# First MLP's output product with half of its k-tiles by Strassen, and a list scheduler for all work behind attention

## The chip, the cores and the metric

The kernel runs on one core of a Trainium2 chip. The metric is device time of one execution in microseconds (us). Of the core's engines five matter here: TensorE (PE in the rows; the weight loads that it does beside its matmuls are PEld), VectorE (DVE), ScalarE (ACT) and SyncE (SP), whose queue issues nearly all transfers from and to the chip's memory (DMA). GpSimd (POOL) does almost nothing.

## The reference, cut to what matters

Attention with a sigmoid in place of a softmax, then two MLPs. Tokens: 2 x 448 = 896; model width 768; the first MLP is 1536 wide, the second 2048.

```python
attn = 1 / (1 + exp(-(q @ k.T / 8 - log(448))))      # 2 x 12 heads, 448 x 64 each
x    = (attn @ v), heads side by side                 # 896 x 768
xn   = x / sqrt(mean(x * x) + 1e-6) * rms_g
h    = silu(xn @ w_gate) * (xn @ w_val)               # 896 x 1536
y    = h @ w_out                                      # 896 x 768   <- the product that changes
g    = silu(y @ w_in)                                 # 896 x 2048
out  = g @ w_out2                                     # 896 x 768
```

## The kernel before

**Numbers.** Every fp32 operand is held as two parts of TensorE's faster fp32 form, high and low. A high part is a copy on ScalarE (`high`, L132), a low part a subtraction on VectorE (`low`, L135). One tile product is three passes (`PASSES`): high x high, high x low, low x high. Activations lie with features on the 128 partitions and the 896 tokens along the row, so that one matmul has 128 x 128 weights and 448 moving columns (one half b of the tokens).

**Weights.** They lie in the chip's memory as 64-bit floats, 6 (in the last product 5) tiles of 128 x 128 to a slab. `load_next` (L124) brings a slab into one of two `raw` buffers. `front` (L137) makes a 32-bit float of it: ScalarE takes the upper word (L145), VectorE or ScalarE the upper bits of the lower word (L151 or L148), VectorE merges them (L153). `back_std` (L160) makes high and low parts in one of 4 `ring` buffers. `back_mac` (L173) does it for two slabs that a Strassen product uses: four sums of blocks (L180, L182, L192, L196) and 3.5 slabs of high and low parts.

**Strassen.** A call of `strassen` (L363) makes two output tiles (256 features) from 6 k-tiles with 7 groups of 9 matmuls (`group`, L346; matmuls on L350) where the plain form has 72. The groups are A11, S1, S2, A12, S3, S4, A22; they use three PSUM banks x, y, z. Between them ScalarE saves partial sums (L380, L382, L385) and VectorE adds them (L372): S2 can write bank x when the first save is done, S3 when the third save is, and A22 when VectorE has added the result of S3. The activations come in seven forms, four blocks (three of them used alone) and four differences of blocks T1 to T4, each again high and low.

**Stages behind attention.** (1) g and v: gate and value of the first MLP, pair by pair; the results are the six h tiles. (2) o: the first MLP's output product, plain, `duo` and `product` (L310, matmuls on L321), 6 output tiles with 12 k-tiles each. (3) i: the second MLP's input product, the pair i0 plain, the pairs i1 to i7 by Strassen. (4) e: the output product, three pairs, each with 6 of 16 k-tiles by Strassen and 10 plain (`mixed`, L405).

**What sets the order.** Each engine runs its instructions in the order in which the program issues them. TensorE's are issued as the loops above stand. VectorE's and ScalarE's side work comes from two sources, the stream of weight steps (`stream`, L247) and a list `fore` of activation work. After each tile or group `pump` (L285) issues from them in turn, as long as a running sum of VectorE's costs stays behind a running sum of TensorE's; the outputs of the products are issued at their place in the loops. ScalarE's costs are not counted. Factors (`PACE_I` and so on) stretch VectorE's costs stage by stage.

Of the kernel before, what the change touches and what calls it, by code (L numbers as in the profile page):

```python
# [21 lines left out]
P = 128  # L22
# [10 lines left out]
PACE_I = 0.85  # L33
PACE_E = 0.85
PACE_M = 1.0
PACE_L = 1.5
POLITE_E = False
# [5 lines left out]
ORDER = (0, 2, 4, 1, 3, 5)  # L43


@with_exitstack
def tile_attention_two_mlps(
# [9 lines left out]

# [30 lines left out]
    items += [("std", first + s) for s in range(KD * K1 // 6)]  # L106
    first += KD * K1 // 6
# [11 lines left out]
    live = {"ring": 0, "w4": 0, "f": 0}  # L119
# [3 lines left out]

    def load_next():  # L124
        if order:
            s = order.pop(0)
            raws[s] = wraw.tile([P, 2 * SLAB], U32, tag="raw", name=f"raw{s}")
            n = 2 * wide(s)
            nc.sync.dma_start(raws[s][:, :n], wd[s].bitcast(U32)[:, :n])
# [7 lines left out]
    def front(s, act_z):  # L137
        while live["f"] >= 3:
            yield None
        yield 0.0  # L140
        live["f"] += 1
        words = raws.pop(s)[:, : 2 * wide(s)].rearrange("p (n two) -> p n two", two=2)
        f = floats[s] = wf.tile([P, SLAB], F32, tag="f", name=f"f{s}")[:, : wide(s)]
        fu = f.bitcast(U32)
        nc.scalar.activation(f, words[:, :, 1].bitcast(F32), AF.Prelu, scale=2.0**-112, alpha=2.0**32)  # L145
        z = words[:, :, 0]
        if act_z:
            nc.scalar.activation(z.bitcast(I32), z, AF.Copy, scale=2.0**-29 * (1 - 2.0**-18), bias=-0.5 + 2.9e-5)  # L148
        else:
            yield 0.56  # L150
            nc.vector.tensor_scalar(z, z, 29, None, ALU.logical_shift_right)  # L151
        yield 0.96
        nc.vector.scalar_tensor_tensor(fu, fu, 3, z, ALU.logical_shift_left, ALU.bitwise_or)  # L153
        load_next()

    def slot(kind, most):
        while live[kind] >= most:
            yield None

    def back_std(s):  # L160
        yield from slot("ring", RING)
        yield 0.0
        live["ring"] += 1
        t = ring.tile([P, 2, SLAB], F32R, tag="w", name=f"w{s}")
        f = floats.pop(s)
        n = wide(s)
        high(t[:, 0, :n], f)
        yield 0.96
        low(t[:, 1, :n], f, t[:, 0, :n])
        live["f"] -= 1  # L170
        wt[s] = t

    def back_mac(s):  # L173
        f, g = floats.pop(s), floats.pop(s + 1)
        a11, a12, a21, a22 = f[:, :HALF], f[:, HALF:], g[:, :HALF], g[:, HALF:]
        tt = nc.vector.tensor_tensor
        yield 0.56
        sums = wsum.tile([P, SLAB], F32, tag="s", name=f"s{s}")
        s1, s2 = sums[:, :HALF], sums[:, HALF:]
        tt(s1, a21, a22, ALU.add)  # L180
        yield 0.56
        tt(s2, s1, a11, ALU.subtract)  # L182
        w = []
        for n in range(2):
            yield from slot("ring", RING)
            yield 0.0
            live["ring"] += 1
            w.append(ring.tile([P, 2, SLAB], F32R, tag="w", name=f"w{s}_{n}"))
            high(w[n][:, 0], (f, sums)[n])
            if n == 0:  # L190
                yield 0.56
                tt(a21, a11, a21, ALU.subtract)  # L192
                yield 0.96
                low(w[0][:, 1], f, w[0][:, 0])
                yield 0.56
                tt(a12, a12, s2, ALU.subtract)  # L196
        yield from slot("ring", RING)
        yield 0.0
        live["ring"] += 1
        w.append(ring.tile([P, 2, SLAB], F32R, tag="w", name=f"w{s}_2"))  # L200
        high(w[2][:, 0], g)
        yield 0.96
        low(w[1][:, 1], sums, w[1][:, 0])
        yield from slot("w4", 1)
        yield 0.0
        live["w4"] += 1
        w4 = wsum.tile([P, 2, HALF], F32R, tag="w4", name=f"w{s}_3")
        high(w4[:, 0], a12)
        yield 0.96
        low(w[2][:, 1], g, w[2][:, 0])  # L210
        yield 0.56
        low(w4[:, 1], a12, w4[:, 0])
        live["f"] -= 2
        wt[s] = {
            "A11": w[0][:, :, :HALF],
            "A12": w[0][:, :, HALF:],
            "S1": w[1][:, :, :HALF],
            "S2": w[1][:, :, HALF:],
            "S3": w[2][:, :, :HALF],
            "A22": w[2][:, :, HALF:],  # L220
            "S4": w4,
        }

    def alternate(a, b):

        gens = [[g, next(g, StopIteration)] for g in (a, b) if g is not None]
        gens = [e for e in gens if e[1] is not StopIteration]
        i = 0
        while gens:
            i %= len(gens)  # L230
            for j in range(len(gens)):
                e = gens[(i + j) % len(gens)]
                if e[1] is None:
                    e[1] = next(e[0])
                if e[1] is not None:
                    break
            else:
                yield None
                continue
            yield e[1]  # L240
            e[1] = next(e[0], StopIteration)
            i = gens.index(e) + 1
            if e[1] is StopIteration:
                gens.remove(e)
                i -= 1

    def stream():  # L247
        before = None
        for kind, s in items:
            act_z = kind == "mac" and s < 2 * K1  # L250
            yield from alternate(front(s, act_z), before)
            if kind == "mac":
                yield from front(s + 1, act_z)
            before = (back_mac if kind == "mac" else back_std)(s)
        yield from before

    steps = stream()
    head = [next(steps)]
    fore, turn, polite, pace = [], [True], [False], [1.0]
    spare = []  # L260

    def unblocked():
        return not fore[0][2:] or bool(spare)

    clock = {"pe": 0.0, "dve": 0.0}

    def step():

        if head[0] is None:
            head[0] = next(steps, StopIteration)  # L270
        can = head[0] is not None and head[0] is not StopIteration
        if fore and unblocked() and not (can and (polite[0] or turn[0])):
            turn[0] = True
            cost, do = fore.pop(0)[:2]
            clock["dve"] += cost * pace[0]
            do()
            return True
        turn[0] = False
        if not can:
            return False  # L280
        clock["dve"] += head[0] * pace[0]
        head[0] = next(steps, StopIteration)
        return True

    def pump():  # L285
        clock["dve"] = max(clock["dve"], clock["pe"] - 3.0)
        while True:
            ahead = [c for c in (fore[0][0] if fore and unblocked() else None, head[0]) if c not in (None, StopIteration)]
            if ahead and clock["dve"] + min(ahead) > clock["pe"]:
                return  # L290
            if not step():
                return

    def evac(cost):
        clock["dve"] = max(clock["dve"], clock["pe"]) + cost

    def until(ready):
        while not ready():
            assert step()

    def weights(s):
        until(lambda: s in wt)
        return wt[s]

    def done(s, n=1):
        live["ring"] -= n
        del wt[s]


    def product(ps, tiles, acts, bs, last=True, after=None, first=True, final=True):  # L310

        n = len(tiles)
        ps = ps if isinstance(ps, list) else [ps[:, b, :S] for b in range(2)]
        for i, (w, a) in enumerate(zip(tiles, acts)):
            s, o = divmod(w, 6)
            fin = o == wide(s) // P - 1
            until(lambda: a in act)
            t, x = weights(s)[:, :, o * P : (o + 1) * P], act[a]
            for step_, (jw, jx) in enumerate(PASSES):
                for b in bs:  # L320
                    nc.tensor.matmul(  # L321
                        ps[b],
                        t[:, jw],
                        x(jx)[:, b * S : (b + 1) * S] if len(x(jx).shape) == 2 else x(jx)[:, b],
                        start=(first and i == 0 and step_ == 0),
                        stop=(final and i == n - 1 and step_ == 2),
                        skip_group_check=True,
                    )
            clock["pe"] += 0.2027 * 3 * len(bs)
            if last and fin:  # L330
                done(s)
# [724 lines left out]
```

## Time and profile before

| what | value |
|---|---|
| time, median of 3 runs | 547.66 us (547.58 to 549.15) |
| the profiled execution's own time | 548.62 us |
| its span, first to last instruction | 546.4 us |
| TensorE busy | 541.0 us, 99% |
| VectorE busy | 388.3 us, 71% |
| ScalarE busy | 315.6 us, 58% |
| DMA, mean over the span | 119 GB/s |
| granted clock of TensorE | 0.999 of full |

The chain that ended last is TensorE for 97% of the span. In the rows below a matmul's own duration is longer than the distance to the next one, since matmuls are pipelined; VectorE's and ScalarE's rows overlap a little in the same way. What an instruction costs its engine is therefore read from start to start.

### The profile page before, as it was taken

What the parts mean: (1) busy time and instruction counts of PE and PEld (TensorE: products, weight loads), DVE (VectorE), ACT (ScalarE), POOL (GpSimd) and SP (SyncE); (2) the same over time, 40 slices, a digit from 0 to 9 for tenths busy, and PEclk for the clock granted to TensorE, in tenths of its full rate; (3) what the DMA queues carried; (4) which work ended last, traced back from release to release, by engine and by line L of the source; (5) the groups of instructions that cost most, each with busy time, mean ns of one, the idle gap of its engine ahead of it and who ended that gap; (6) DMA issues with size and microseconds to landing.
All of it is one profiled execution on the core that took longest, in us unless ns stands there. A gap on an engine that the chain in (4) does not pass through costs nothing.

```text
span 546.4 us, 7105 instructions
## 1 busy us (share of the span) xinstructions
PE 541.0 (99%) x2785; PEld 468.8 (86%) x2785; DVE 388.3 (71%) x589; ACT 315.6 (58%) x438; POOL 0.2 (0%) x4
## 2 busy tenths in 40 slices
PE   8999999999999999999999999999999999999997
PEld 4555459999999999999999999999999899999996
DVE  4576777897777877899563587599989995835610
ACT  5887773656757585757353355577767945223400
POOL 0000000000000000000000000000000000000000
PEclk9999999999999999999999999999999999999999
DMA  8855100443333333335533330233333443714201
GB/s 277 287 176 161 58 1 0 140 150 115 117 116 116 116 116 115 117 115 175 173 116 115 116 116 6 111 115 116 116 108 101 150 152 107 244 47 128 83 22 47
DMA packets 15521, 65.00 MB, mean 119 GB/s; under 512 B 1984, under 2 KB 3776, under 8 KB 15488
## 3 DMA queue, kind: packets, MB, share of 16 engines
q1 hardware_dynamic: 15344, 64.32, 35.7%
q8 instruction: 22, 0.36, 0.3%
q10 hardware_dynamic: 144, 0.23, 0.1%
q14 instruction: 11, 0.09, 0.1%
HBM read 61.79 MB, written 2.75 MB: 118 GB/s over the span
## 4 chain that ended last, share of the span: by engine, by line
PE 97%; ACT 1%; DMA 1%; issue 0%; DVE 0%
PE o L321 16%; PE av L533 7%; PE sc L517 6%; PE v L321 5%; PE g L321 3%; PE i L321 3%; PE e0b L321 2%; PE e1b L321 2%; PE e1a L321 2%; PE e0a L321 2%; PE e0x L350 1%; PE i6x L350 1%; PE e2x L350 1%; PE i3x L350 1%; PE v3x L350 1%; PE i5x L350 1%
## 5 line engine op out<-in xcount | busy, mean ns | idle before, releaser
L132 ACT ACTIVATE w<-f 128x768 fp32r<-128x768 f32 (+2 forms) x89 | 67.5, 762 | 66.5 <-PE o L321 22.7
L135 DVE TENSOR_TENSOR w<-f,w 128x768 fp32r<-128x768 f32 (+2 forms) x89 | 74.2, 849 | 40.9 <-ACT w L132 40.9
L153 DVE SCALAR_TENSOR_TENSOR f<-f,raw 128x768 uint32<-128x768 uint32 (+1 forms) x70 | 65.3, 932 | 19.7 <-ACT raw L148 14.0
L145 ACT ACTIVATE f<-raw 128x768 f32<-128x768 f32 (+1 forms) x70 | 61.4, 888 | 25.6 <-DMA raw<-in_w 20.6
L321 PE MATMUL o<-hhi,w 128*128 128x448 f32 x288 | 70.2, 365 | 0.0
L321 PEld LDWEIGHTS o<-hhi,w 128*128 128x128 f32 x288 | 54.1, 188 | 4.3
L525 ACT ACTIVATE a<-sc,logs 112x896 f32<-112x896 f32 x48 | 45.0, 1012 | 6.0 <-PE sc L517 5.7
L321 PE MATMUL o<-hlo,w 128*128 128x448 f32 x144 | 40.9, 365 | 0.0
L533 PE MATMUL av<-a,vr 112*64 112x448 f32 x192 | 39.4, 547 | 0.0
L517 PEld LDWEIGHTS sc<-ks 64*112 64x112 f32 x288 | 25.5, 181 | 14.2 <-ACT a L525 8.5
L517 PE MATMUL sc<-ks 64*112 64x448 f32 x288 | 35.0, 388 | 0.6 <-ACT ks L507 0.6
L321 PE MATMUL v<-x,w 128*128 128x448 f32 x144 | 29.9, 368 | 0.0
L533 PEld LDWEIGHTS av<-a,vr 112*64 112x64 f32 x192 | 12.3, 136 | 20.3 <-issue 18.2
L151 DVE TENSOR_SCALAR raw<-raw 128x768 uint32<-128x768 uint32 (+1 forms) x52 | 28.1, 540 | 2.0 <-DMA raw<-in_w 1.9
L321 PEld LDWEIGHTS v<-x,w 128*128 128x128 f32 x144 | 27.1, 188 | 2.5 <-issue 0.4
L321 PEld LDWEIGHTS o<-hlo,w 128*128 128x128 f32 x144 | 27.1, 188 | 2.1
L132 ACT ACTIVATE w<-s 128x768 fp32r<-128x768 f32 x19 | 16.0, 841 | 10.2 <-PE o L321 4.8
L135 DVE TENSOR_TENSOR w<-s,w 128x768 fp32r<-128x768 f32 x19 | 18.0, 949 | 3.1 <-ACT w L132 3.1
L148 ACT ACTIVATE raw<-raw 128x768 int32<-128x768 uint32 x18 | 16.1, 897 | 0.0
L321 PE MATMUL g<-x,w 128*128 128x448 f32 x72 | 15.3, 369 | 0.0
L321 PEld LDWEIGHTS g<-x,w 128*128 128x128 f32 x72 | 13.4, 188 | 1.8 <-issue 0.7
L321 PE MATMUL i<-y,w 128*128 128x448 f32 x72 | 14.8, 365 | 0.0
(443 smaller groups left out, 1051.5 us busy)
## 6 DMA issues: line engine op xcount, KB each, us to landing
raw<-in_w SPq DMA_DIRECT2D x58, 768.0 KB, 4.3
raw<-in_w SPq DMA_DIRECT2D x12, 640.0 KB, 3.9
kq<-in_kq SPq DMA_DIRECT2D x11, 448.0 KB, 6.0
vr<-in_v SPq DMA_DIRECT2D x12, 224.0 KB, 4.8
out_t<-e0s SPq DMA_DIRECT2D x4, 224.0 KB, 3.0
out_t<-e1s SPq DMA_DIRECT2D x4, 224.0 KB, 1.9
out_t<-e2s SPq DMA_DIRECT2D x4, 224.0 KB, 1.9
kq<-in_kq ACTq DMA_DIRECT2D x1, 224.0 KB, 3.5
```

The lines of the kernel that those rows point to most:

```text
L132: nc.scalar.activation(dst, src, AF.Copy)
L135: nc.vector.tensor_tensor(dst, src, hi.bitcast(F32), ALU.subtract)
L145: nc.scalar.activation(f, words[:, :, 1].bitcast(F32), AF.Prelu, scale=2.0**-112, alpha=2.0**32)
L148: nc.scalar.activation(z.bitcast(I32), z, AF.Copy, scale=2.0**-29 * (1 - 2.0**-18), bias=-0.5 + 2.9e-5)
L151: nc.vector.tensor_scalar(z, z, 29, None, ALU.logical_shift_right)
L153: nc.vector.scalar_tensor_tensor(fu, fu, 3, z, ALU.logical_shift_left, ALU.bitwise_or)
L321: nc.tensor.matmul(ps[b], t[:, jw], x(jx)[:, b * S : (b + 1) * S] if len(x(jx).shape) == 2 else x(jx)[:, b], start=(first and i == 0 and s ...
L350: nc.tensor.matmul(ps, w[a][:, jw, t * P : (t + 1) * P], forms(b, t, jx), start=(start and t == 0 and n == 0), stop=(stop and t == 2 and n ...
L517: nc.tensor.matmul(ps[:CP, h, :S], ks[i][rows, jk, 0, c * CP : (c + 1) * CP], ks[i][rows, jq, 1, :], start=(step == 0), stop=(step == 2),)
L525: nc.scalar.activation(a, ps[:CP, :, :S], AF.Sigmoid, bias=logs[:CP], scale=D**-0.5)
L533: nc.tensor.matmul(ps[h * D : (h + 1) * D], vr[i][:, c, h, :], a[:, h, :], start=(c == 0), stop=(c == NC - 1),)
```

## The change

**The product o** is now made like e: `mixed` is called for three pairs of output tiles with h tiles 0 to 2 (6 k-tiles) by Strassen and h tiles 3 to 5 (6 k-tiles) plain. For the first two pairs the plain part comes first, for the third it comes last. The three h tiles need their blocks and differences (`formed`: 5 high parts, 5 low parts and 4 subtractions where a plain tile has 2 and 2), and six of o's slabs go through the Strassen form of the weights. The outputs are added into the fp32 tiles `yr` (`dest`), and `y_put` makes high and low parts from there, half by half.

**The order** is no longer made by `pump`. Everything behind attention becomes a `Job` with an engine, a cost, its inputs and what it takes from a stock (ring buffers, PSUM banks and so on). `Plan.run` walks through time with one queue per engine: TensorE's jobs keep their order, every other engine takes the startable job with the earliest due date, which is worked back from when TensorE would need its result. The costs are formulas of the row length. The slabs' bit step is on ScalarE for o as well now (`ZO`). Activation tiles come from one store that is given back half by half. In attention itself only the names and homes of small tiles change, and two weight steps less are done there. SyncE's queue has the same 70 slab loads and 12 output transfers as before, in nearly the same sequence.

```diff
-    pair = duo("o", w0, K1, "h")
-    for m in range(2, KD):
-        product(ps, range(w0, w0 + K1), [("h", k) for k in range(K1)], (0, 1), after=after)
-        collected(m, ps, [(both, ps[:, :, :S])])
+    keys = [("h", k) for k in range(6, K1)]
+    for t in range(3):
+        dest = lambda m, b, t=t: r2[t]()[:, b, m]
+        if t < 2:
+            weight_std(s, ZO)
+            weight_std(s + 1, ZO)
+            weight_mac(s + 2, ZO)
+            mixed(f"o{t}", s + 2, s, keys, 6, hbook, hdep, y_put(t), dest)
+        else:
+            weight_mac(s, ZO)
+            weight_std(s + 2, ZO)
+            weight_std(s + 3, ZO)
+            mixed(f"o{t}", s, s + 2, keys, 6, hbook, hdep, y_put(t), dest, ahead=False, own=hown)
+        s += 4
...
+LAG = {"A": 0.105, "D": 0.081, "P": 0.165, "S": 4.4}
+HOP = 0.6
...
+    def dve(n, fn, deps=(), **more):
+        return plan.add("D", 0.071 + n / 960, fn, deps, **more)
+    def scalar(n, fn, deps=(), psum=False, **more):
+        return plan.add("A", (0.072 if psum else 0.109) + n / 1215, fn, deps, **more)
+    def tensor(n, fn, deps=(), **more):
+        return plan.add("P", 0.2027 * n, fn, deps, **more)
...
+    def run(self, busy):
...
+        t = 0.0
+        for j in self.pe:
+            j.due = t
+            t += j.cost
+        for j in reversed(self.jobs):
+            if j.eng != "P":
+                j.due = min([u.due for u in j.users + j.users_of_gift], default=1e9) - j.cost - LAG[j.eng] - HOP
...
+        def pick(e, now):
...
+            for j in sorted(pool[e], key=lambda j: j.due):
+                if not startable(j, now):
+                    continue
+                late = now + j.cost
+                if any(now < u.ready < late and u.due + drift < late and u.due < j.due for u in pool[e]):
+                    continue
+                return j
...
+    def y_put(t):
+        def put(m, b, src, dep):
...
+            l = dve(S, lo_, [scalar(S, hi_, [dep], need=some)])
...
+            if len(ydone[t]) == 4:
+                turned("y", t, r2[t], ydone[t], ybook[t], ydep[t], yown[t])
...
+    def formed(key, q, tile_, deps, book, fdep, own):
...
+        for name, src in (("B11", b11), ("B21", b21), ("B22", b22)):
...
+            h_ = scalar(S, raw, deps, need=some)
+            lows.append(dve(S, raw_low, [h_]))
...
+        t1, t2, t3, t4 = differences(blocks, lows)
...
+        ls = split(f"{key}{q}t", srcs, [[t1, t3], [t2, t4]], keep, lambda: tile_.back(keep_))
```

Three places of the new order follow, each beside the old one.

The first is TensorE in the product o. Before, every row is a pair of matmuls of one plain k-tile of output tile o2 (its weights are `w28`):

```order
L321 MATMUL o2_2485<-hhi0_2157,w28_2344 128x448 x2
L321 MATMUL o2_2485<-hlo0_2172,w28_2344 128x448 x2
L321 MATMUL o2_2485<-hhi0_2157,w28_2344 128x448 x4
L321 MATMUL o2_2485<-hlo0_2172,w28_2344 128x448 x2
L321 MATMUL o2_2485<-hhi0_2157,w28_2344 128x448 x2
```

Now the pair o0 goes from its last plain tile (L678) to its Strassen groups (L726; `w26_0` and `w26_1` are two of the four parts of a Strassen weight, `h2B11` and `h2th0` forms of h tile 2):

```order
L678 MATMUL o0b_2277<-x3_87,w25_2212 128x448 x2
L678 MATMUL o0b_2277<-x1h1_1119,w25_2212 128x448 x2
L678 MATMUL o0b_2277<-x3_87,w25_2212 128x448 x2
L726 MATMUL o0x_2376<-x2l1_1204,w26_0_2299 128x448 x3
L726 MATMUL o0x_2376<-h0tl1_1371,w26_0_2299 128x448 x3
L726 MATMUL o0x_2376<-h2B11_1661,w26_0_2299 128x448 x3
L726 MATMUL o0y_2396<-x0_84,w26_1_2334 128x448
L726 MATMUL o0y_2396<-x2_86,w26_1_2334 128x448
L726 MATMUL o0y_2396<-x0_84,w26_1_2334 128x448
```

In all, o has 405 matmuls where it had 432; nothing else on TensorE changes in number.

The second is ScalarE in the last pair of the input product, i7. Before, the saves `i7s0`, `i7s1`, `i7s2` stand with two 896-wide copies and, once, a slab's first step between them:

```order
L380 ACTIVATE i7s0_3662<-i7x_3659 128x448
L132 ACTIVATE y0_2471<-g2_3_3206 128x2x448
L132 ACTIVATE y2_2580<-g2_3_3206 128x2x448
L145 ACTIVATE f54_3696<-raw54_3598 128x640
L382 ACTIVATE i7s1_3663<-i7y_3660 128x448
L132 ACTIVATE y1_0_2824<-g2_4_3319 128x2x448
L132 ACTIVATE y2_0_2910<-g2_4_3319 128x2x448
L385 ACTIVATE i7s2_3664<-i7x_3659 128x448
```

Now (L759 is a save):

```order
L759 ACTIVATE i7s0_3756<-i7x_3730 128x448
L256 ACTIVATE h0tl1_1371<-g2_4_3480 128x896
L266 ACTIVATE f54_3765<-raw54_3671 128x640
L759 ACTIVATE i7s1_3770<-i7y_3748 128x448
L794 ACTIVATE g2_6_3696<-i6x_3621 128x448
L759 ACTIVATE i7s2_3786<-i7x_3730 128x448
```

One copy is left between the first two saves, and a 448-wide SiLU stands between the second and the third.

The third is VectorE between the pairs i1 and i2, up to the first addition of i2 that waits for TensorE (`g2_2<-i2z`). Before:

```order
L372 TENSOR_TENSOR g2_1_3003<-i1y_3005,i1s2_3009 128x448
L135 TENSOR_TENSOR w40_2_3061<-f41_2949,w40_2_3061 128x768
L135 TENSOR_TENSOR w40_3_3085<-f40_2774,w40_3_3085 128x384
L151 TENSOR_SCALAR raw43_2965<-raw43_2965 128x768
L153 SCALAR_TENSOR_TENSOR f43_3107<-f43_3107,raw43_2965 128x768
...
L135 TENSOR_TENSOR w42_0_3132<-f42_2967,w42_0_3132 128x768
L196 TENSOR_TENSOR f42_2967<-f42_2967,s42_3115 128x384
L135 TENSOR_TENSOR e0_2883<-g2_0_2886,e0_2883 128x448 x2
L135 TENSOR_TENSOR e1_2884<-g2_0_2886,e1_2884 128x448
L372 TENSOR_TENSOR g2_2_3090<-i2z_3093,i2s0_3094 128x448
```

Now:

```order
L765 TENSOR_TENSOR g2_1_3126<-i1y_3069,i1s2_3109 128x448
L259 TENSOR_TENSOR g0tl0_3158<-g2_0_3009,y4_1_2912 128x896
L278 SCALAR_TENSOR_TENSOR f43_3149<-f43_3149,raw43_3041 128x768
...
L278 SCALAR_TENSOR_TENSOR f44_3192<-f44_3192,raw44_3051 128x768
L259 TENSOR_TENSOR g1B11_3213<-g2_0_3009,g0tl0_3158 128x896
L259 TENSOR_TENSOR g1B11_3213<-g2_1_3126,g1B11_3213 128x448
L270 TENSOR_SCALAR raw45_3177<-raw45_3177 128x768
L259 TENSOR_TENSOR g1B21_3222<-g2_1_3126,g1B21_3222 128x448
L765 TENSOR_TENSOR g2_2_3246<-i2z_3218,i2s0_3190 128x448
```

The forms of g tiles 0 and 1 (`g0t`, `g1B`) now stand here, 896 and 448 wide, where before three narrow rows did.

## Rows read from the trace of the kernel before

**Rows 1.** the page's head and its part on busy time

```profile
span 546.4 us, 7105 instructions
...
PE 541.0 (99%) x2785; PEld 468.8 (86%) x2785; DVE 388.3 (71%) x589; ACT 315.6 (58%) x438; POOL 0.2 (0%) x4
```

**Rows 2.** the chain that ended last, from 239 us on: start us, us, what

```profile
239.64 87.55 PE o L321 x432
...
354.55 1.82 PE i2x L350 x9
...
431.50 2.43 PE e0a L321 x12
...
542.84 0.62 DVE e2s L454
```

**Rows 3.** who TensorE waited for, whole span: us, times, longest us

```profile
PE idle L637 <- DVE logs L645: 1.1, 1, 1.1
PE sc L517 <- ACT ks L507: 0.6, 1, 0.6
```

**Rows 4.** stages g and v, o, i, e: length, PE, PEld, DVE, ACT, POOL busy, PEclk, DMA

```profile
95.54:239.64 144.10, 144.10 (x713) 133.62 (x712) 116.13 (x171) 95.92 (x136) 0.00 (x0) 1.00 0.36 121
239.64:327.19 87.55, 87.55 (x433) 81.16 (x433) 59.49 (x76) 40.78 (x52) 0.00 (x0) 1.00 0.41 135
327.19:431.50 104.31, 104.24 (x514) 96.28 (x514) 88.19 (x134) 72.90 (x108) 0.00 (x0) 1.00 0.31 101
431.50:542.82 111.32, 111.30 (x549) 102.73 (x548) 62.28 (x93) 38.69 (x56) 0.00 (x0) 1.00 0.33 106
```

**Rows 5.** TensorE in i7, by start: start us, us, what

```profile
423.71 1.98 PE L350 MATMUL i7z<-y,w 128*128 128x448 f32 x9
425.76 2.09 PE L350 MATMUL i7x<-y,w 128*128 128x448 f32 x9
```

**Rows 6.** ScalarE in i5 and i7, by start

```profile
405.23 0.51 ACT L132 ACTIVATE w<-f 128x384 fp32r<-128x384 f32 x1
...
423.47 1.80 ACT L132 ACTIVATE y<-g 128x896 fp32r<-128x896 f32 x2
425.16 0.55 ACT L385 ACTIVATE i7s<-i7x 128x448 f32<-128x448 f32 x1
```

**Rows 7.** VectorE in i5 and i6, by start

```profile
395.73 0.56 DVE L151 TENSOR_SCALAR raw<-raw 128x768 uint32<-128x768 uint32 x1
396.20 0.55 DVE L182 TENSOR_TENSOR s<-s,f 128x384 f32<-128x384 f32 x1
396.67 0.95 DVE L153 SCALAR_TENSOR_TENSOR f<-f,raw 128x768 uint32<-128x768 uint32 x1
397.54 0.55 DVE L192 TENSOR_TENSOR f<-f,f 128x384 f32<-128x384 f32 x1
...
401.32 0.61 DVE L372 TENSOR_TENSOR g<-i5z,i5s 128x448 f32<-128x448 f32 x1
401.86 0.95 DVE L135 TENSOR_TENSOR w<-s,w 128x768 fp32r<-128x768 f32 x1
...
405.77 0.56 DVE L135 TENSOR_TENSOR w<-f,w 128x384 fp32r<-128x384 f32 x1 [0.45 <-ACT w L132]
...
412.82 1.08 DVE L135 TENSOR_TENSOR gl<-g,gl 128x896 fp32r<-128x896 f32 x1
413.82 0.62 DVE L372 TENSOR_TENSOR g<-i6z,i6s 128x448 f32<-128x448 f32 x1
```

**Rows 8.** VectorE at the end of v5, by start

```profile
234.20 0.62 DVE L374 TENSOR_TENSOR v5s<-v5z,v5s 128x448 f32<-128x448 f32 x1 [0.33 <-PE v5z L350]
234.86 0.62 DVE L376 TENSOR_TENSOR h<-h,v5s 128x448 f32<-128x448 f32 x1
```

**Rows 9.** ScalarE's copies of slabs, from the costliest groups of the page

```profile
L132 ACT ACTIVATE w<-f 128x768 fp32r<-128x768 f32 (+2 forms) x89 | 67.5, 762 | 66.5 <-PE o L321 22.7
```

**Rows 10.** transfers of whole slabs, from the page's part on DMA

```profile
raw<-in_w SPq DMA_DIRECT2D x58, 768.0 KB, 4.3
```

More of the change, by code (lines that the diff above doesn't have):

```diff
@@ L43, with __init__, then @@
 ORDER = (0, 2, 4, 1, 3, 5)
+class Job:
+    def __init__(self, eng, cost, fn, deps, take, need):
+        self.eng, self.cost, self.fn, self.take, self.need = eng, cost, fn, take, need
+        self.deps = [d for d in deps if d is not None]
+        self.users, self.users_of_gift, self.ends = [], [], []
+        self.due, self.ready, self.left = 1e9, 0.0, 0
+        for d in self.deps:
+            d.users.append(self)
+    def then(self, fn):
+        self.ends.append(fn)
+        return self
@@ L156, in slot @@
[L156 to L263, printed above, removed]
@@ L285, in pump @@
[L285 to L331, printed above, removed]
-            if after:
-                after(i)
-            if not lead:
-                pump()
@@ new lines, in tensor, with new, some, any_whole @@
+    def tensor(n, fn, deps=(), **more):
+        return plan.add("P", 0.2027 * n, fn, deps, **more)
+    whole, part, reserve = [], {}, [0]
+    def new(tag, dtype, name, n=2):
+        return pools[tag[0]].tile([P, n, 2, S], dtype, tag=tag, name=name)
+    def some():
+        return bool(part) or len(whole) > reserve[0]
+    def any_whole():
+        return bool(whole)
+    def half(name):
+        if part:
+            tag = next(iter(part))
+            h = part[tag].pop(0)
+            if not part[tag]:
+                del part[tag]
+            return h
+        tag = whole.pop(0)
+        t = new(tag, F32R, name)
+        part[tag] = [(tag, t[:, 1])]
+        return tag, t[:, 0]
@@ new lines, in give, with give_all, full, weight_front @@
+    def give(h):
+        tag = h[0]
+        part.setdefault(tag, []).append(h)
+        if len(part[tag]) == 2:
+            del part[tag]
+            whole.append(tag)
+    def give_all(hs):
+        for h in hs:
+            give(h)
+    def full(name):
+        tag = whole.pop(0)
+        return tag, new(tag, F32, name)
+    whole += [f"T{n}" for n in range(6)] + ["e0", "e1"]
+    part["e2"] = [("e2", new("e2", F32R, "half", 1)[:, 0])]
+    wjob = {}
+    def weight_front(s, act_z):
+        n = wide(s)
+        r = None if s in LOADED else plan.add("S", 0.4, lambda: load(s), take="raw")
+        e = scalar(1.08 * n, lambda: exponent(s), [r], take="f")
+        z = scalar(1.07 * n, lambda: tail_act(s), [r]) if act_z else dve(n / 2, lambda: tail_dve(s), [r])
+        return plan.frees("raw", dve(n, lambda: merge(s), [e, z]))
@@ new lines, in split, with hi_, lo_ @@
+    def split(name, srcs, deps, own, done):
+        got = {}
+        def hi_(n):
+            got[n] = [half(f"{name}h{n}")]
+            high(got[n][0][1], srcs[n]())
+        def lo_(n):
+            got[n].append(half(f"{name}l{n}"))
+            low(got[n][1][1], srcs[n](), got[n][0][1])
+            own(n, *got[n])
+        hs = [scalar(NT, lambda n=n: hi_(n), deps[n], need=some) for n in range(len(srcs))]
+        ls = [dve(NT, lambda n=n: lo_(n), [hs[n]], need=some) for n in range(len(srcs))]
+        plan.after_all(ls, done)
+        return ls
@@ L989, in tile_attention_two_mlps @@
[L989 to L995 removed]
+                ps = Banks(f"i{m}", True)
+                tiles = range(6 * (s + m), 6 * (s + m) + 6)
+                e = product([ps.bank(b) for b in range(2)], tiles, [("y", k) for k in range(KD)], (0, 1), take="ps", start=ps.start)[-1]
```

1003 lines of the change are left out of this document (597 added, 406 removed).

## The prediction

> **What bounds the kernel now.** I read the page's head first: TensorE is busy for 541.0 of 546.4 us [rows 1]. Then the chain that ended last, to see what that busy time is: from 239 us to the last matmul it is matmuls one behind the other, and only VectorE's last copy and the output transfer come behind [rows 2]. Then who TensorE waited for: two waits at the start, 1.7 us in all, and nothing later [rows 3]. Then the busy time by stage, to see what the other engines have left. From 95.54 to 542.82 us PE works 447.20 of 447.28 us at the full clock; VectorE is at 81% in g and v, 68% in o, 85% in i and 56% in e [rows 4]. So TensorE's number of matmuls sets the time, and VectorE in the stage i is the engine that could take over.
>
> **What is removed.** The chain gives o 87.55 us for 432 matmuls, 0.2027 us each [rows 2]. A Strassen group of 9 takes 1.82 us, a plain step of 12 takes 2.43 us [rows 2]: 0.2022 and 0.2025 us each, so a matmul costs the same in either form. A pair of output tiles took 144 matmuls; it now takes 63 in seven groups and 72 plain, 7 x 1.82 + 6 x 2.43 = 27.32 us against 29.18. Three pairs: 82.0 instead of 87.55 us, a gain of 5.5 us (27 matmuls x 0.2027 = 5.47). All of it lies on the path.
>
> A second, small term: in i7 the third group's bank is freed by ScalarE's save `i7s2`, which stood behind two 896-wide copies (423.47 to 425.27) and ended at 425.71 [rows 6]. TensorE's group i7z began at 423.71 and the next one 2.05 us later, not 1.82 [rows 5]: 0.23 us lost. In the new order a 448-wide SiLU stands before this save, at 0.55 us like the save itself [rows 6]; so the 0.2 us should go.
>
> **What is added, and what it lies beside.** Counted in the order of both kernels. VectorE gets 46 rows more of 448 columns (forms of three h tiles, outputs added out of PSUM, low parts half by half), 15 more of 384 and 3 more of 768 (weight sums), 4 fewer of 896, and 12 bit steps fewer, which go to ScalarE. The price of a row is the time from its start to the next start: 0.54 us for 448 columns, 0.47 for 384, 0.87 for 768, 1.00 for 896 [rows 7]; 0.47 for a bit step [rows 7]. Sum: 24.8 + 7.1 + 2.6 - 4.0 - 5.6 = +24.9 us. VectorE had 447.3 - 326.1 = 121 us to spare behind attention [rows 4]. ScalarE gets 42 rows more and 8 wide ones fewer; at 0.76 us, the mean of its slab copies [rows 9], the 42 are at most 32 us, against 447.3 - 248.3 = 199 us to spare. Nothing of this is on the path as long as each result is there before its group.
>
> Where it goes matters more than the sum. By stage (cut at the last rows of v5, of o and of i7) the new order has on VectorE 121.0 us of rows in g and v (98.5 before), 70.3 in o (71.0), 89.0 in i (82.0), 54.9 in e (59.5), by the same prices. TensorE's new stages are 144.1, 82.0, about 104 and 111 us. So o itself stays at 86% although it is shorter, since h tiles 0 and 1 are prepared in g and v; and i comes to 86% of 104 us.
>
> **Three places walked by hand.** (1) v5 to o0. From VectorE's last output of v5, which waits for the last group, to the last form that o0's second group needs (h tile 2's T1) 17 rows stand in the order, itself included: 12.2 us by the prices above. TensorE needs that form 14.6 us of plain steps, a group of 1.82 and two thirds of a group later, 17.6 us: 5.4 us in hand. (2) i1 to i2. From the addition of `i1y` to that of `i2z` VectorE has 9.05 us of rows, before 8.9; TensorE is 5 groups, 9.1 us, from one to the other. VectorE arrives at the very moment, as it did before, when i2's groups followed each other without a gap [rows 2]. Being late does not yet cost: group A22 waits only for the addition of `i2x`, and between that addition and A22 lies a whole group of 1.82 us. (3) i7. In the new order a low part of g tile 4 waits for the second tile of i7's A12 before it may use its place, and the addition of `i7z` stands behind it. That addition then ends about 1 us late, and the one of `i7x`, behind two more rows, still comes 0.9 us ahead of A22. The same form (a low part that waits for a place) stands before v5's A22, with 0.5 us in hand. These two are the narrowest places I found; each can lose some tenths, bounded by 0 and by one wide row, 1.0 us [rows 7].
>
> A hand-over costs next to nothing: a copy on ScalarE ended at 405.74 and VectorE's row that waited for it began at 405.77 [rows 6, 7]. A VectorE row that needs the row right before it starts 0.66 us after it instead of 0.54 [rows 8]. The list scheduler allows 0.6 us for each hand-over between engines, so the real engines arrive earlier than the order supposes, and early arrival costs nothing in an in-order queue.
>
> SyncE's transfers are the same in number. A Strassen pair needs two slabs in 12.8 us, a load lands in 4.3 us [rows 10], and there are two buffers; I cost them at nothing. In attention, the start and the last copy I see no edit that TensorE would feel; I allow 0.3 us either way.
>
> [...]Here rows overlap: a 448-wide addition started at 401.32, lasted 0.61 us, and the next row started at 401.86 [rows 7]. [...]
>
> **Sum.** The profiled execution took 548.62 us; 548.62 - 5.5 - 0.2 = 542.9. The median of the runs is 0.96 us below the profiled one, so I forecast 542.0, with 541.2 to 543.2 as this case's own range.
>
> **Rivals.**
> - *Stalls at the hand-overs.* v5's A22, o0, i2 to i4 and i7 are met with less than a group in hand. If four or five of them lose 0.3 to 1.0 us (one wide row), 1.2 to 5 us of the gain go: 543.2 to 547, typically 544. For: stage i has VectorE rows without a gap for 9 us. Against: before it was nearly as dense and lost only 0.2 us [rows 4, 5]. Chance 0.15.
> - *VectorE becomes the bound of i: slower.* Before, i left VectorE 104.3 - 88.2 = 16.1 us idle, waiting for ScalarE and TensorE [rows 4]. With 7.0 us of rows more it is busy for 95.2 us. If an in-order queue cannot do without the idle time of before, the stage takes 95.2 + 16.1 = 111.3 us, 7.0 more than before, and the kernel 547.66 - 5.5 + 7.0 = 549.2. It begins to cost when more than 104.1 - 95.2 = 8.9 us of idle time stay, and from 14.4 us the gain is gone. Against: the new order fills waits with whatever is due next. A kin of it: if rows did not overlap, each would be 0.08 us dearer (0.62 for 0.54 [rows 7]), 140 x 0.08 = 11.2 us; the rows of i would take 89.0 + 11.2 = 100.2 of 104 us, and with half of the old idle time, 8 us, the stage would be 4.1 us longer: 547.66 - 5.5 + 4.1 = 546.3. Chance 0.04 and 0.01.
> - *The product does not get cheaper in time*, because its new forms of h come late: o0's second group would wait until they are there. The 5.4 us in hand of place (1) must be gone first, by h tile 2 being ready later than I think; to lose all the gain it takes another 5.5 us on top, 547.5. Chance 0.04.
> - *More gain than the count:* there is little to win, since TensorE waits 0.08 us by the records behind 95 us [rows 4]. Under 541.2: chance 0.03.
>
> **How the numbers follow.** Forecast 0.73, stalls 0.15, slower 0.05, no cheaper 0.04, more 0.03. The range 541.0 to 545.0 takes in the forecast and most of the stalls. A difference under 0.3% (1.6 us) cannot be told from none here: faster means below 546.0, slower above 549.3. Faster: 0.73 + 0.03 + nearly all of the stalls = 0.89; same: the rest of the stalls, "no cheaper" and a part of the slower case = 0.07; slower: 0.04.
>
> **What would show it.** In the profile after: o in 82 us and no gap between its groups; i7's third group 1.82 us behind the one before; VectorE busy some 25 us longer, above 85% from o to i; no entry of an o, i or e line among TensorE's waits above some tenths. I am wrong if a group in v5, o0 or i waits for VectorE or ScalarE by more than 1 us, or if a matmul of the new o costs more than 0.203 us.

## The result, and the profile after

| kernel | median, us | runs | ratio to before, 95% interval |
|---|---|---|---|
| before | 548.4 | 547.58 to 550.65 | |
| after | 542.27 | 541.37 to 543.13 | 0.988 (0.984 to 0.992) |

The forecast was 542.0 with a range of 541.0 to 545.0. The kernel is 1.2% faster, well beyond the 0.3% that can be told from no change.

The page's head of the profiled execution (it took 541.37 us), as in [rows 1]:

```profile
span 539.4 us, 7085 instructions
...
PE 534.2 (99%) x2758; PEld 462.2 (86%) x2758; DVE 407.7 (76%) x637; ACT 332.9 (62%) x472; POOL 0.2 (0%) x4
```

27 matmuls fewer; VectorE busy 19.4 us longer, ScalarE 17.3. TensorE stays at 99%. The chain that ended last (start us, us, what), against [rows 2]:

```profile
238.49 2.44 PE o0a L678 x12
...
253.08 1.82 PE o0x L726 x9
...
320.57 14.60 PE i L678 x72
...
424.54 2.43 PE e0a L678 x12
...
535.84 0.62 DVE e2s L878
```

o runs from 238.49 to 320.57: 82.08 us where it took 87.55. Its six plain tiles of the first pair (`o0a`, `o0b`) take 14.6 us, and the first Strassen group `o0x` follows at once, so the new forms of h tile 2 were there. i takes 103.97 us (104.31 before), e up to its last copy 111.30 (111.34). Who TensorE waited for, against [rows 3]:

```profile
PE idle L487 <- DVE logs L495: 1.1, 1, 1.1
PE sc L366 <- ACT ks L356: 0.3, 1, 0.3
```

Nothing behind attention. The stages g and v, o, i and e (length, then PE, PEld, DVE, ACT and POOL busy, PEclk, DMA), against [rows 4]:

```profile
94.40:238.49 144.09, 144.09 (x712) 133.52 (x712) 121.63 (x184) 104.21 (x151) 0.00 (x0) 1.00 0.33 110
238.49:320.57 82.08, 82.08 (x406) 76.06 (x406) 72.79 (x110) 49.97 (x70) 0.00 (x0) 1.00 0.43 145
320.57:424.54 103.97, 103.97 (x514) 96.34 (x514) 88.46 (x137) 71.81 (x109) 0.00 (x0) 1.00 0.30 102
424.54:535.84 111.30, 111.26 (x549) 102.76 (x548) 60.41 (x90) 38.26 (x55) 0.00 (x0) 1.00 0.32 106
```

VectorE is busy for 89% of o and 85% of i. That mean hides what matters in i. Its plain pair i0 and the Strassen pairs i1 to i5, with the same columns:

```profile
320.57:335.16 14.59, 14.59 (x73) 13.52 (x73) 11.46 (x16) 6.77 (x9) 0.00 (x0) 1.00 0.13 50
335.16:347.93 12.77, 12.77 (x65) 11.84 (x64) 10.95 (x18) 9.66 (x15) 0.00 (x0) 1.00 0.16 67
347.93:360.70 12.77, 12.77 (x64) 11.83 (x64) 12.46 (x21) 10.12 (x17) 0.00 (x0) 1.00 0.38 124
360.70:373.47 12.77, 12.77 (x64) 11.84 (x64) 12.52 (x22) 9.30 (x16) 0.00 (x0) 1.00 0.37 124
373.47:386.24 12.77, 12.77 (x64) 11.83 (x64) 12.52 (x21) 8.74 (x14) 0.00 (x0) 1.00 0.36 124
386.24:399.00 12.76, 12.76 (x64) 11.82 (x64) 9.67 (x16) 8.00 (x13) 0.00 (x0) 1.00 0.34 114
```

In i0 and i1 VectorE has 3.1 and 1.8 us free, in i2 to i4 only 0.3 us each (98% busy), and in i5 3.1 us again: the forms of the first g tiles are made in i2 to i4.

**Where the 6.1 us come from.** The start varies from run to run by over a microsecond, also for one and the same kernel. These rows are the first gate matmuls behind attention in the chain (start us, us, what). The two profiles of before:

```profile
79.13 3.90 PE g L321 x18
```

```profile
78.44 3.85 PE g L321 x18
```

The two of after:

```profile
77.99 3.83 PE g L678 x18
```

```profile
79.37 3.83 PE g L678 x18
```

So I count from that matmul to the end of the profiled run's time: before 548.62 - 79.13 = 469.49 and 547.90 - 78.44 = 469.46; after 541.37 - 77.99 = 463.38 and 542.76 - 79.37 = 463.39. This measure repeats to 0.03 us, and it is 6.1 us shorter: o 5.47 (82.08 for 87.55), i 0.34, e 0.04, and some 0.2 outside the span (2.2 us outside it before, 2.0 after). I call it "from the first g" below. Matmul starts that are compared below are taken from one view each.

### The profile page after: what moved, and what is told of

It reads as the page before. It is cut to its first block, busy times and chain, and to the rows that moved or that the text cites. A ratio compares the mean times of both kernels' runs of the same rounds, so it can differ in the third digit from the quotient of the medians.

```text
span 539.4 us, 7085 instructions
## 1 busy us (share of the span) xinstructions
PE 534.2 (99%) x2758; PEld 462.2 (86%) x2758; DVE 407.7 (76%) x637; ACT 332.9 (62%) x472; POOL 0.2 (0%) x4
## 4 chain that ended last, share of the span: by engine, by line
PE 98%; DMA 1%; DVE 0%; ACT 0%; issue 0%
PE av L382 7%; PE sc L366 6%; PE v L678 5%; PE g L678 3%; PE i L678 3%; PE e1b L678 2%; PE e1a L678 2%; PE e0b L678 2%; PE e0a L678 2%; PE v2x L726 1%; PE e2x L726 1%; PE i5x L726 1%; PE o1b L678 1%; PE o0b L678 1%; PE g5x L726 1%; PE e1x L726 1%
## 5 line engine op out<-in xcount | busy, mean ns | idle before, releaser
L259 DVE TENSOR_TENSOR w<-f,w 128x768 fp32r<-128x768 f32 (+2 forms) x92 | 76.7, 839 | 17.8 <-ACT w L256 17.6
L366 PEld LDWEIGHTS sc<-ks 64*112 64x112 f32 x288 | 23.9, 171 | 14.7 <-ACT a L374 7.7
L678 PE MATMUL v<-x,w 128*128 128x448 f32 x144 | 29.9, 368 | 0.0
L678 PEld LDWEIGHTS v<-x,w 128*128 128x128 f32 x144 | 27.0, 188 | 2.5 <-issue 0.4
L270 DVE TENSOR_SCALAR raw<-raw 128x768 uint32<-128x768 uint32 (+1 forms) x40 | 21.3, 538 | 9.6 <-DMA raw<-in_w 9.6
L274 ACT ACTIVATE raw<-raw 128x768 int32<-128x768 uint32 x30 | 26.9, 903 | 0.9 <-DMA raw<-in_w 0.9
L256 ACT ACTIVATE w<-s 128x768 fp32r<-128x768 f32 x22 | 18.5, 839 | 9.6 <-PE e1a L678 5.2
L259 DVE TENSOR_TENSOR w<-s,w 128x768 fp32r<-128x768 f32 x22 | 20.9, 950 | 3.8 <-ACT w L256 3.8
L794 ACT ACTIVATE g<-g 128x448 f32<-128x448 f32 (+1 forms) x14 | 10.7, 764 | 9.0 <-DVE g L765 9.0
L678 PE MATMUL g<-x,w 128*128 128x448 f32 x72 | 15.3, 368 | 0.0
L678 PEld LDWEIGHTS g<-x,w 128*128 128x128 f32 x72 | 13.4, 188 | 1.8 <-issue 0.7
L678 PE MATMUL i<-y,w 128*128 128x448 f32 x48 | 13.5, 365 | 0.0
L349 DVE CAST ks<-kq 128x896 fp32r<-128x896 f32 x11 | 6.9, 623 | 7.6 <-PE sc L366 5.4
L642 DVE TENSOR_TENSOR s<-s,f 128x384 f32<-128x384 f32 x22 | 12.2, 553 | 0.2
L350 DVE TENSOR_TENSOR ks<-kq,ks 128x896 fp32r<-128x896 f32 x11 | 12.0, 1092 | 0.4
```

The costliest lines, as they stand in the source:

```text
L256: nc.scalar.activation(dst, src, AF.Copy)
L259: nc.vector.tensor_tensor(dst, src, hi.bitcast(F32), ALU.subtract)
L366: nc.tensor.matmul(ps[:CP, h, :S], ks[i][rows, jk, 0, c * CP : (c + 1) * CP], ks[i][rows, jq, 1, :], start=(step == 0), stop=(step == 2),)
L642: s2 = dve(HALF, lambda: tt(sums[0][:, HALF:], sums[0][:, :HALF], block(0), ALU.subtract), [s1, m[0]])
L678: nc.tensor.matmul(banks[b](), t[:, jw], act[key](jx, b), start=(first and i == 0 and n_ == 0), stop=(final and i == n - 1 and n_ == 2), s ...
```

## The experiments

My theory: the number of matmuls sets the time, and VectorE's and ScalarE's work is hidden as long as each result comes before its group. The rivals: the scheduler itself gives a part; attention does; VectorE is close to being the bound.

| run | median, us | ratio to before, 95% | from the first g, us |
|---|---|---|---|
| before again | 547.77 | 0.9995 (0.9985 to 1.0004) | 469.46 |
| after again | 542.12 | 0.9872 (0.9858 to 0.9886) | 463.39 |
| o plain, scheduler kept | 547.24 | 0.9973 (0.9963 to 0.9983) | 468.95 |
| i0 by Strassen | 547.60 | 0.9996 (0.9973 to 1.0018) | 468.70 |
| i0 by Strassen, early forms | 539.77 | 0.9833 (0.9821 to 0.9846) | 461.58 |
| one row more per pair | 543.18 | 0.9910 (0.9893 to 0.9927) | 464.5 |
| two rows more | 547.41 | 0.9992 (0.9977 to 1.0008) | 468.6 |
| three rows more | 552.77 | 1.0082 (1.0058 to 1.0105) | 471.7 |
| three rows, i1 to i3 only | 544.97 | 0.9955 (0.9924 to 0.9987) | 466.78 |
| three rows, i5 to i7 only | 542.48 | 0.9881 (0.9866 to 0.9896) | 464.42 |
| no due dates | 551.08 | 1.0042 (1.0021 to 1.0064) | 473.68 |
| no hand-over allowance | 542.36 | 0.9890 (0.9865 to 0.9916) | 464.11 |

### Both kernels again

No edit.

> The changed kernel once more, as the yardstick for the kernels timed beside it. By my count (27 matmuls fewer of 0.2027 us, 0.2 us of waiting gone in i7) its ratio to before is 0.989, 541.9 to 542.6 us beside 547.7 to 548.5. In the first profiles attention was 1.1 us shorter than before, although TensorE's order in it is the same. Theory T: that part is chance of the start and a second profile shows it anywhere between 77.9 and 79.2 us for the end of the last av. Rival: the two weight steps fewer in attention shorten it, and it ends at 78.0 again.

> The kernel before once more, for its attention: the end of the last av matmul stood at 79.13 us in its first profile, at 77.99 and 79.37 in the two of the changed kernel. Theory T (chance of the start): anywhere from 77.9 to 79.4; the ratio to before is 1.000 within 0.002. Rival (the two weight steps more in its attention cost 1 us): 79.1 again or later.

The first g stood at 79.37 us in the changed kernel (0.2 us later than I had allowed) and at 78.44 in the one before: the other way round than in the first profiles. So the 1.1 us of the first profiles were chance, and attention gives nothing that can be told from its scatter.

### The scheduler alone

Matmuls, weights and h tiles of o as before, everything ordered by the scheduler (m is the output tile of a pair, each with 12 k-tiles):

```diff
-            formed("h", p - 1, f[p - 1], fdone[p - 1], hbook[p - 1], hdep[p - 1], hown[p - 1])
+            halved("h", p - 1, f[p - 1], fdone[p - 1], hrest)
...
+    def plain(t, s, dest):
+        for m in range(2):
+            weight_std(s + 2 * m, ZO)
+            weight_std(s + 2 * m + 1, ZO)
...
+            e = product([ps.bank(b) for b in range(2)], tiles, [("h", k) for k in range(K1)], (0, 1), take="ps", start=ps.start)[-1]
...
-        if t < 2:
+        if True:
+            plain(t, s, dest)
+        elif t < 2:
```

> The list scheduler alone: o is plain again (432 matmuls, 12 k-tiles per output tile), all six h tiles are split into a high and a low part, and everything else is still ordered by the scheduler. Theory T (the number of matmuls sets the time, the order hides the rest as well as before): 27 x 0.2027 = 5.5 us above the changed kernel, about 547.7, so 0.1 to 0.8 us under the kernel before; o takes 87.5 us. Rival, the scheduler itself brings a part: under 546.5. Rival, the scheduler is worse than the old pump and Strassen pays for it: above 548.8.

547.24 us, 5.1 above the changed kernel by medians and 5.56 from the first g. Its chain (start us, us, what):

```profile
238.80 87.56 PE o L678 x432
326.35 14.59 PE i L678 x72
...
430.32 2.44 PE e0a L678 x12
```

o is back at 87.55 us (238.80 to 326.35), i stays at 103.97 (326.35 to 430.32). So Strassen is worth its 27 matmuls, and the scheduler alone 0.5 us from the first g, 0.34 of it in i. The rival that it brings more falls. Whether the old order would have hidden the new rows of VectorE and ScalarE as well was not tested: no kernel here has o by Strassen without the scheduler.

### The pair i0 by Strassen

```diff
-        reserve[0] = 6
+        reserve[0] = 7
...
-        if p == 0:
-            weight_std(s, False)
-            weight_std(s + 1, False)
...
-        else:
+        if True:
             weight_mac(s, False)
             gdone[p] = strassen(f"i{p}", s, ybook, ydep, g2[p], yown if p == NP2 - 1 else None)
```

The part of each y tile that only the plain pair used is no longer made.

> The pair i0 of the second MLP's input product by Strassen too (63 matmuls in place of 72), all else ordered by the scheduler as before. It takes away the 14.6 us of plain matmuls that stand between o's last group and the first pair that needs the forms of y tile 2. Theory T (a hand-over costs what the chain of side work is longer than the matmuls that cover it): in the changed kernel the low part of y2's first forms ends at 326.9 us, 6.4 us after o's last matmul began to be followed by i0; the second group of i0 would need it at 1.82 + 1.22 us after, 323.4. So TensorE waits 2.5 to 3.5 us for it and saves 1.82: 0.7 to 1.7 us slower than the changed kernel, 543.0 to 544.0. Rival, matmuls alone set the time: 1.8 us faster, 540.4. Rival, the whole of i is thrown back because VectorE has more to do in it: over 545.

547.60 us: 5.5 slower than the changed kernel, where I expected 0.7 to 1.7. TensorE by start (start us, us, what, idle before it and its releaser):

```profile
323.24 0.36 PE L725 MATMUL i0y<-x2l,w 128*128 128x448 f32 x1
326.64 0.74 PE L725 MATMUL i0y<-x,w 128*128 128x448 f32 x1 [3.04 <-ACT x L255]
328.47 0.74 PE L725 MATMUL i0y<-half,w 128*128 128x448 f32 x1 [1.08 <-DVE half L258]
...
329.38 0.57 PE L725 MATMUL i0x<-y,w 128*128 128x448 f32 x1
...
334.83 0.37 PE L725 MATMUL i0x<-y,w 128*128 128x448 f32 x1
```

The waits are where they were expected and are 3.04 + 1.08 us, some 0.6 to 1.6 more. But the rows behind show matmuls that last 0.57 us, and in the windows (columns as above) the granted clock fell:

```profile
320.00:326.50 6.50, 3.60 (x18) 3.01 (x16) 6.19 (x12) 2.72 (x5) 0.00 (x0) 1.00 0.29 112
326.50:333.30 6.80, 5.57 (x14) 4.60 (x15) 3.48 (x5) 1.79 (x4) 0.00 (x0) 0.50 0.34 116
333.30:340.00 6.70, 6.70 (x35) 6.22 (x34) 4.29 (x6) 4.00 (x7) 0.00 (x0) 1.00 0.01 2
```

It was 0.50 of full, 1.2 GHz, from 326.5 to 333.3: it fell at the end of the wait of 3.04 us and came back 6.7 us after TensorE had begun again. In a dense row the matmul behind that of 323.24 would have started at 323.44; from there to 334.83 it took 11.4 us for 21 matmuls that need 4.26 at full clock. Of the 7.1 us too much 4.1 are waiting; the other 3.0 I put down to the lower clock, at which matmuls stand 0.37 us apart. 7.1 - 1.8 = 5.3, what was measured from the first g. The number lies where the last of my expectations put it, but not for its reason: from i1 to the end of i it takes 89.4 us as before. The clock was in none of them.

### The pair i0 by Strassen, with early forms

As above, and the forms of y tile 2 one by one:

```diff
-            if len(ydone[t]) == 4:
+            if t == 2 and len(ydone[t]) == 4:
+                turned_early("y", t, r2[t], yat[t], ybook[t], ydep[t], yown[t])
+            elif len(ydone[t]) == 4:
                 turned("y", t, r2[t], ydone[t], ybook[t], ydep[t], yown[t])
...
+        t1 = dve(S, sub(b11, b12, b11), [at_[0, 0], at_[0, 1]])
+        form("T1", 0, 0, b11, [t1])
+        t3 = dve(S, sub(b12, b22, b12), [t1, at_[1, 1]])
+        t2 = dve(S, sub(b22, b22, b11), [t3])
+        form("T2", 1, 1, b22, [t2])
+        form("T3", 1, 0, b12, [t3])
+        t4 = dve(S, sub(b21, b21, b22), [t2, at_[1, 0]])
+        form("T4", 0, 1, b21, [t4])
```

> As the kernel with i0 by Strassen, but y tile 2's four differences and their high and low parts are made one by one, 448 wide, each as soon as its own blocks are there, where they waited for all four blocks and went two by two. The first difference then needs only outputs that end 7.3 us before o does. Theory T (the wait at the hand-over is the only price): no group of i0 waits, 9 matmuls fewer, 1.8 us faster than the changed kernel: 540.4, 540.0 to 540.9. Rival, VectorE's extra rows in i (a third denser than g and v) bind: no faster than the changed kernel.

539.77 us, 1.81 less than the changed kernel from the first g. Its chain:

```profile
320.81 1.83 PE i0x L725 x9
...
422.95 2.43 PE e0a L677 x12
```

i takes 102.14 us (320.81 to 422.95) for 103.97, and no line of i stands among TensorE's waits. It is the fastest version here, 1.7% under before.

### More rows for VectorE, the order unchanged

Low parts of the weights are made twice in the pairs i1 to i7; `again` is (0,), (0, 1) or (0, 1, 2), and the scheduler's costs don't know of it:

```diff
         def lower(n):
-            low(w[n][:, 1], src(n)(), w[n][:, 0])
+            for _ in range(1 + (n in again)):
+                low(w[n][:, 1], src(n)(), w[n][:, 0])
```

> More VectorE work in the stage i without a change of order: in each of the 7 Strassen pairs one 768-wide low part of the weights is made twice (the same numbers again, right behind the first time; the scheduler isn't told). 7 x 0.87 = 6.1 us more; VectorE's rows in i come from 89.0 to 95.1 of 104.0 us. Theory T (VectorE's work is hidden until its rows fill the stage): 542.1 to 542.7, as the changed kernel; a wait of some tenths may show. Rival, VectorE's idle time in i can't be dispensed with (in the changed kernel 103.97 - 88.46 = 15.5 us of it): i grows by what is added, 548. Between them, a wait of over 2 us and then a lower granted clock behind it, as behind the wait of i0 by Strassen, where 4.1 us of waiting were followed by some 6 us at half clock: 544 to 547.

> As before, two of the low parts made twice in each pair: 12.2 us more, VectorE's rows in i come to 101.2 of 104.0 us. Theory T: the rows still fit, but the 9 us between i1 and i2 that had nothing to spare now are 1.7 us too long, and so every pair's 12.8 us hold 12.4 us of rows: TensorE waits several times by some tenths, 0 to 4 us in all, 542 to 546, more if the clock falls behind a wait. Rival (idle time can't be dispensed with): 554.

> All three low parts made twice in each pair: 18.3 us more, VectorE's rows in i come to 107.3 us and no longer fit into 104.0. Theory T: VectorE is the bound of i; the stage takes at least 107.3 us, 3.3 more, and with the waits that stay and the clock behind them 546 to 552. Rival (idle time can't be dispensed with): 560. Rival, TensorE alone sets the time whatever VectorE does: 542.

Added 6.1, 12.2 and 18.3 us; from the first g it became 1.1, 5.2 and 8.3 us longer, by medians 1.0, 5.2 and 10.6 (one profiled run each stands behind the first figures). All three medians lie above what theory T allowed (542.1 to 542.7, 542 to 546, 546 to 552). Neither the room of the whole stage (15.5 us: nothing should show before the third dose) nor a fixed share of idle time (6, 12, 18 us) fits. Where TensorE waited (us in total, times, longest), with two rows more:

```profile
PE i3x L727 <- DVE g L766: 1.4, 1, 1.4
PE i2x L727 <- DVE g L766: 1.3, 1, 1.3
...
PE i4x L727 <- DVE g L766: 1.1, 1, 1.1
```

and with three:

```profile
PE i2x L727 <- DVE g L766: 2.1, 1, 2.1
PE i3x L727 <- DVE g L766: 2.0, 1, 2.0
...
PE i4x L727 <- DVE g L766: 0.7, 1, 0.7
```

Only i2 to i4 stand in these lists, each before its A22, for the addition. i5 to i7 take 38.3 us with one and with two rows more, as without. So VectorE bound i2 to i4 and no others as far as these lists go.

With three rows more the clock takes part too. It was at half for 3.4 us from the end of the wait in i3 on (columns as above):

```profile
377.70:381.10 3.40, 3.30 (x9) 2.96 (x10) 3.37 (x7) 1.99 (x4) 0.00 (x0) 0.50 0.00 0
```

By the distances of its matmuls this is some 1.5 of the 8.3 us. The profiled run is the fastest of the four (550.70 us), and all four have a mean granted clock of 0.994 to 0.997; the others have no trace.

### The same work early and late

```diff
-            weight_mac(s, False)
+            weight_mac(s, False, (0, 1, 2) if p in (1, 2, 3) else ())
```

and the same with (5, 6, 7).

> All three low parts of the weights made twice, but only in the pairs i1, i2 and i3: 3 x 2.61 = 7.8 us of VectorE's work more, in the order of the changed kernel. In the changed kernel VectorE is busy for 10.95, 12.46 and 12.52 us in these pairs of 12.77 each, so 2.4 us are free, and 15.5 in the whole of i. Theory T (the room counts pair by pair): 7.8 - 2.4 = 5.4 us more, 547 to 548, up to 1 us on top where the clock falls behind a wait; the waits stand before A22 of i2 to i4. Rival (the room of the whole stage counts): 542.1 to 542.7.

> The same 7.8 us of VectorE's work more, but in the pairs i5, i6 and i7, where VectorE is busy for 9.67, 9.30 and 9.59 of 12.77 us each: 9.7 us free. Theory T (the room counts pair by pair): hidden, 542.1 to 542.7, at most 1 us more by a single wait in i7. Rival (a fixed share of idle time cannot be used, about 10 us in i): 547 to 550. Rival (the room of the whole stage counts): 542.1 to 542.7 as well; this one is told apart by the same rows in i1 to i3.

7.8 us more in each. For i1 to i3 it costs 3.4 us from the first g (2.8 by medians), for i5 to i7 1.0 (0.3). The place counts and not the sum; but I had expected 5.4 for the early ones. The waits show the reason. Early:

```profile
PE i2x L727 <- DVE g L766: 2.1, 1, 2.1
...
PE i3x L727 <- DVE g L766: 0.2, 1, 0.2
```

Late:

```profile
PE i4x L727 <- DVE g L766: 0.5, 1, 0.5
```

The weights of i1 to i3 make i2 wait, and those of i5 already i4: weights are made a pair ahead of their use. So the early rows fall mostly into i0 to i2, which have 3.1, 1.8 and 0.3 us free: 2.6 us of rows in each are 0, 0.8 and 2.3 us too many, 3.1 in all, against 3.4 measured. I had put them one pair too late. The late rows fall into i4 to i6; by the same count they would cost 2.3 us, all in i4; they cost 1.0. So the place is right, and the size only roughly. That the listed waits are shorter (2.3 us early, 0.5 late) has a reason in the trace: from start to start i loses 3.4 and 1.0 us, since the second matmul behind a wait is 0.1 us late too and waits that are shorter than a matmul's own 0.36 us stand in no list.

### The scheduler's rules

Without due dates (n is a job's number in the order of creation):

```diff
-            for j in sorted(pool[e], key=lambda j: j.due):
+            for j in sorted(pool[e], key=lambda j: j.n):
...
-                if any(now < u.ready < late and u.due + drift < late and u.due < j.due for u in pool[e]):
+                if False:
                     continue
```

Without the allowance:

```diff
-HOP = 0.6
+HOP = 0.0
```

> The changed kernel with the scheduler's due dates taken out: each engine takes the first job that can start, in the order in which the program created them, and keeps no place for a job that becomes ready a little later. The jobs, their costs and TensorE's order are the same. Theory T (where VectorE has 0.3 us free in a pair, the sequence of its rows decides): waits in i2 to i4 and at the hand-overs, 545 or more. Rival (any order that starts what can start will do, since TensorE is the bound by far): 542.1 to 542.7.

> The allowance for a hand-over between engines in the scheduler (0.6 us) set to 0; the trace of before showed 0.03 us for one. VectorE's order changes in many places. Theory T (early arrival costs nothing and so the 0.6 us neither help nor harm): 541.9 to 542.7. Rival (the allowance keeps rows that wait for ScalarE from standing at the head of VectorE's queue, and i2 to i4 have no room for that): 543 to 546. Rival (the true value fits better): under 541.6.

Without due dates more than the whole gain is lost: 551.08 us, 473.68 from the first g, 10.3 more. The edit takes out two rules, the due dates and the place kept for a job that is ready a little later; which of them counts was not tested. Its first waits:

```profile
PE i2x L726 <- DVE g L765: 1.7, 1, 1.7
...
PE i1x L726 <- DVE g L765: 1.1, 1, 1.1
PE o0a L678 <- DVE x L259: 0.8, 1, 0.8
```

The five that are listed behind attention make 4.5 us; from start to start, with the short ones, waits cost 7.6 us more than in the changed kernel. The other 2.7 us come from two stretches, 140 to 243 us and 309 to 344 us, in which matmuls stand further apart:

```profile
226.47 1.86 PE g5x L726 x9
...
326.02 14.89 PE i L678 x72
```

9 matmuls in 1.86 us and 72 plain ones in 14.89, 1.82 and 14.60 in the changed kernel. The allowance of 0.6 us, on the other hand, makes no difference that the medians can tell (542.36); from the first g it is 0.7 us longer without it, 0.6 of it ahead of o.

## Why the prediction was right, step by step

- **Matmuls (step 1).** Forecast 82.0 us for o and 5.5 us of gain; 82.08 and 5.47 measured, 0.2027 us for each of 405 matmuls, and the kernel with o plain gives it back. Right, and for the reason given.
- **The save in i7.** Forecast 0.2 us. TensorE in i7 now, against [rows 5] (start us, us, what; a group is three such rows or more):

```profile
417.08 0.77 PE L726 MATMUL i7z<-y,w 128*128 128x448 f32 x3
...
418.91 0.77 PE L726 MATMUL i7x<-y0h,w 128*128 128x448 f32 x3
```

  The next group comes 1.83 us behind i7z, not 2.05, and i is 0.34 us shorter (before, the second matmul behind this wait was 0.1 us late as well). Right; the kernel with o plain has the same 103.97 us, so it is the order's doing.
- **VectorE's sum, +24.9 us.** 19.4 us measured by busy time: too large by 5.5. My prices are distances in a dense queue, while the busy time of before counts a lonely row at its full 0.62 us; the rows stand denser now. That this is the whole difference was not tested, and nothing of it lies on the path. The slower rival mixed the two measures: it added 7.0 us by dense prices to a busy time of 88.2 and put VectorE at 95.2 us in i, where 88.46 were measured.
- **The walks.** VectorE's rows of the hand-overs by start:

```profile
235.32 0.62 DVE L765 TENSOR_TENSOR v5s<-v5x,v5s 128x448 f32<-128x448 f32 x1
...
346.26 0.62 DVE L765 TENSOR_TENSOR g<-i1y,i1s 128x448 f32<-128x448 f32 x1
346.80 1.08 DVE L259 TENSOR_TENSOR g0tl<-g,y 128x896 fp32r<-128x896 f32 x1
...
355.29 0.62 DVE L765 TENSOR_TENSOR g<-i2z,i2s 128x448 f32<-128x448 f32 x1
...
357.09 0.62 DVE L765 TENSOR_TENSOR g<-i2x,i2s 128x448 f32<-128x448 f32 x1 [0.31 <-PE i2x L726]
...
419.90 0.62 DVE L765 TENSOR_TENSOR g<-i7z,i7s 128x448 f32<-128x448 f32 x1
...
421.57 0.62 DVE L765 TENSOR_TENSOR g<-i7x,i7s 128x448 f32<-128x448 f32 x1
```

(2) i1y's addition to i2z's: 9.03 us (346.26 to 355.29), forecast 9.05; it does arrive with the group's end. The addition of i2x ends at 357.71, 1.0 us before A22. (3) i7z's addition begins 0.9 us after its group's end at 419.0, forecast "about 1 us late"; i7x's ends at 422.19, 0.4 us ahead of A22 (forecast 0.9). (1) T1 of h tile 2 ended at 251.70 and was first used at 255.96: 4.3 us in hand, forecast 5.4, since VectorE came 1 us late to v5's last output. The addition of v5x ends at 235.94, 0.6 us ahead of v5's A22 at 236.51 (forecast 0.5). All of them held, two with less in hand than forecast.
- **Rows that overlap.** A 448-wide row of 0.62 us is followed after 0.54 (346.26 and 346.80). The kin of the slower rival, rows that do not overlap, would add some 0.08 us to each of the 21 rows of i2, 1.7 us to 12.46 of 12.77 us, and TensorE would wait there. It does not.
- **The rivals' prices were wrong**, although none of them came. I counted VectorE's room over the stage, 8.9 us before it costs; it counts pair by pair, and i2 to i4 have 0.3 us each. The change was nearer to a loss in i than I wrote. And I priced a stall at its own length; a long one can also take the clock (3.0 us behind the wait in i0).
- **The sum.** A gain of 5.7 us was forecast; from the first g it is 6.1: the two terms are 5.47 and 0.34, e gives 0.04, and 0.2 lie outside the span, for which no run shows a cause. That the median meets 542.0 within 0.3 us is in part luck: the start alone scatters by over 1 us.

## What to carry to other kernels

Where TensorE is busy all the time, as here, a cut in matmuls is worth its count as long as every hand-over holds; look for the tightest few microseconds, since the mean of a stage does not show them. Split a form's inputs so that each part starts as soon as its own data is there: that turned a loss of 5.3 us into a gain of 1.8 (from the first g). To compare kernels to a tenth, measure from a landmark behind the part that scatters.

## What the runs showed of the hardware

- TensorE's granted clock fell to half at the end of a wait of 3.04 us (i0 by Strassen), and was back at full 6.7 us after TensorE began again (326.64 to 333.3). With three rows more it fell at the end of a wait of 2.0 us in i3, for 3.4 us, while a wait of 2.1 us in i2, 15 us before, left it at full. With waits of 1.1 to 1.4 us (two rows more) the mean granted clock of the profiled run stayed 1.000.
- The kernel with the rows early, which waits 2.1 us in i2, took 544.7 to 545.0 us in seven runs with a mean granted clock of 0.999 to 1.000, and 550.0 to 551.0 in three with 0.995 to 0.997. No trace of the three was taken.
- At a granted clock of 1.00, matmuls stood 0.2068 us apart (14.89 / 72) in two stretches of the kernel without due dates, and 0.2028 (14.60 / 72) in the changed kernel. The second stretch begins behind a listed wait (0.3 us before o2x), and each ends at a wait; the longest two waits of that kernel behind attention (1.7 us in i2 and 1.1 in i1) are not followed by it. No run here says why.
